# A fused attention and mixture-of-experts kernel: second products of three slots with w2 stationary, stored by output group

## The chip, the core and the metric

One core of one Trainium2 chip runs the whole program. The time is in device microseconds (us), and the number to beat is the median of three runs. Five engines work side by side, each through its own instructions in a fixed order: TensorE (PE), VectorE (DVE), ScalarE (ACT), GpSimd (POOL) and SyncE (SP), which here only issues DMAs. PEld is TensorE's weight load.

## The reference

The kernel computes attention with pooled queries and passes its result to a top-1 mixture of experts:

```
q_pool = q.reshape(B, H, S // 2, 2, D).mean(axis=3)      # B=8, H=8, S=1152, D=64
attn   = softmax(q_pool @ k^T / sqrt(D)) @ v
x      = attn as (4608 tokens, 512 features)
expert = argmax(x @ w_gate)                               # 8 experts
gate   = softmax(x @ w_gate)[expert]
out[token] = gate * (relu(x @ w1[expert]) @ w2[expert])   # w1: 512x1024, w2: 1024x512
```

## The kernel before, in words

**Stages.** The attention stage takes some 685 us: scores, exponentials, value products, and after each batch the routing, which writes every token into its expert's list in DRAM (a token number and its gate) and the token's 512 features into `x_runs`, cut into four runs of 128 features (each with 4 scale factors). Then come 16 expert slots, each one expert and up to 372 or 248 tokens: three early slots (31 places in each of 12 blocks), six wide slots with `PLACES` = 31, 29, 29, 27, 24, 24 places in each of 12 blocks of 32 (372, 348, 348, 324, 288 and 288 columns, in that order), and seven static slots with 31 places in 8 blocks (248 columns).

**A slot.** `tokens_of` loads the slot's piece of the list twice through GpSimd's queue (`re`, token and gate by output row, used by the store; `li`, from which `ix`, the indices of the runs, is made) and gathers the rows by indirect DMA, one GpSimd instruction per block, 12 in a wide slot and 8 in a static one (L1019). A gather waits for a mark, a group of matmuls of the slot two before, so that the gathers are spread over that slot. `turn_tokens` scales the rows on VectorE (`weigh`, L1198), turns them in 32 x 32 blocks (L1201), and splits the result into a high part (ScalarE, L1228) and a low part (VectorE, L1162), `xh` and `xl`. `split_weights` does the same for `w1` and `w2`, in four pieces of 1024 elements a partition each (L1245 and L1162). Every product is then three: high by high, high by low, low by high.

**First products** (L1288): a 128 x 128 block of `w1` is stationary, the slot's tokens move; 96 matmuls write the hidden values into `ph`, from where ScalarE makes `hh` (relu, L1296) and VectorE the low part `hl` (L1298). **Second products** (`second_products`, L1304 to L1337): for each group of 128 tokens a block of `hh` or `hl` is stationary and 512 columns of `w2` move; 24 matmuls for a group, 72 for a wide slot, 48 for a static one. ScalarE multiplies `py` by the gate into `y` (L1335), and GpSimd stores the 128 rows of 2 KB by one indirect DMA (L1327). There are two `ph` and two `py` banks, three `y` buffers, one `xh`/`xl`, and one buffer for each piece of the split weights.

**Order.** The program adds steps with a key, a duration and the buffers that they hold. `Flow.emit` plays them through a model (engines, two DMA queues, waits, buffers) and writes each engine's instructions in the order in which the model started them. `carry` adds an issuing step and a DMA step with a time of its own; in the model, DMA steps of GpSimd's queue (`DMA2`) pass one after the other, and a gather there takes 400 ns. On the chip each engine then keeps that order and waits at any instruction whose data is not there.

Of the kernel before, what the change touches and what calls it, by code (L numbers as in the profile page):

```python
# [9 lines left out]
F32 = mybir.dt.float32  # L10
# [9 lines left out]
EARLY = 3  # L20
PLACES = (31, 29, 29, 27, 24, 24)
WIDE = len(PLACES)
STATIC_SLOTS = 7
S_BUFS = 3
# [32 lines left out]
XR = 6  # L57
Y_BUFS = 3
DMA = 2000
# [203 lines left out]
def kernel(  # L263
# [173 lines left out]
    def act(n):  # L437
        return 110 + 0.833 * n

    def dve(n):  # L440
        return 67 + 1.042 * n
# [28 lines left out]
    def done(*steps):  # L470
        return [s for s in steps if s is not None]
# [483 lines left out]

    def tokens_of(o, f, key, tab, s, n, known, stored, early=False, m=None, steps=(), used=BU):

# [3 lines left out]
        x.n = x.nb * used  # L961
        x.whole = early
        x.re = tile_of(o, "rec2", [P, TW // P, 2], bufs=RE_BUFS)
# [10 lines left out]
        def load():  # L974


            src = lists[bass.ds(entry(tab, s, NE * LIST, ET_), n), :].rearrange("(i b) c -> i (b c)", b=x.nb)
            ins = [eng.dma_start(out=x.re.t[:x.rt, :x.nr].rearrange("p r c -> p (r c)"),
                                     in_=src[:x.u].rearrange("i (g r) -> g i r", g=NQD)),
# [47 lines left out]
        def mark(i):  # L1027
            return steps[i * len(steps) // x.nb] if steps else None

        p = f.carry(at, 2600, load, key - LEAD, [*known, *stored], [x.re, x.li], 120)  # L1030
        p = f.add("POOL", 250, index, key - LEAD, done(p), [x.li, x.ix])
        x.rows = done(*(f.carry("POOL", 1310, lambda i=i: gather(i), key + i * 3 / x.nb, done(p, mark(i) and mark(i).step, *stored), [x.ix, x.xr[i // NQD]], 400)
                        for i in range(x.nb)))
# [152 lines left out]
    def turn_tokens(o, m, f, x, key):  # L1186
# [4 lines left out]
        for r in range(x.nr):  # L1191
# [31 lines left out]

            p = f.add("DVE", dve(DM), weigh, key + r, x.rows[r * NQD:(r + 1) * NQD], [x.xr[r]])
            p = f.add("DVE", dve(DM), turn, key + r, done(p), [xt, x.xr[r]])
# [8 lines left out]
    def split_weights(m, f, x, kind, key, step, pool_bits):  # L1234
# [7 lines left out]
        for j in range(4):  # L1242
            src = lambda j=j: raw[j].t.rearrange("p (c f) -> p c f", c=NDC if one else 2)
            e = "POOL" if pool_bits >> j & 1 else "DVE"
            a = f.add("ACT", act(1024), lambda j=j, src=src: nc.scalar.copy(w[j].t[0], src()),  # L1245
                      key + step * j, done(got[j]), [raw[j], w[j]])
# [16 lines left out]
    def first_products(o, m, f, x, key):  # L1263
# [7 lines left out]
        for f0 in range(0, NFC, nb):  # L1271
            ph = hold_of("ph", lambda h: m.ps.tile([P, 512], F32, **h.own("ph")))
            view = lambda ph=ph: ph.t[:, :nb * n].rearrange("p (b t) -> p b t", b=nb)
            apart = lambda ph=ph: ph.t[:, :nb * n].rearrange("p (b t) -> p b t", t=x.rt)
            home = lambda i, f0=f0: blocks(hidden(m)[i])[:, f0 * x.nr:(f0 + nb) * x.nr, :x.rt]
            fs = slice(f0, f0 + nb)
# [27 lines left out]
    def second_products(o, m, f, x, key):  # L1304

        for r in range(x.nr):
# [30 lines left out]
            f.carry("POOL", 1300, scatter, at, done(a), [y, x.re], 1200)  # L1337


    with ExitStack() as cm, ExitStack() as units, ExitStack() as pairs:  # L1340
# [3 lines left out]
        def swap_units():  # L1344
# [4 lines left out]
                      fold=FOLD_BUFS, pa=1, sm=2, xT=2, rec=2, row=ROW_BUFS, lw=1, ex=1, de=1,  # L1349
                      ohb=1, di=2, re=2, rec2=RE_BUFS, li=LI_BUFS, ix=LI_BUFS, xr=XR, xq=XR2, xt=XT, raw=RAW, x=1, **{f"{w}{j}": 1 for w in ("w1", "w2") for j in range(4)}, **{f"h{c}": 1 for c in range(NFC)}, ph=2, py=2, px=2, y=Y_BUFS),  # L1350
                 ("kT", "qT", "vn", "fold", "s", "st"), ("x", "xt", "xq", *(f"{w}{j}" for w in ("w1", "w2") for j in range(4)), *(f"h{c}" for c in range(NFC)), "ph", "py", "px", "y"), swap_units)
        hold = []
# [36 lines left out]
        flag(o, f, key + K_SLOT + 20, [*outs, *table])  # L1389
        order = [(early, i, TW) for i in range(EARLY)] + [(wide, i, TW) for i in range(WIDE)]  # L1390
        order += [((etab, rtab), i, T) for i in range(STATIC_SLOTS)]
        base, marks = key + K_SLOT, []
        for i, (tab, s, n) in enumerate(order):
            at = base + SLOT * i
            experts, places_ = tab if isinstance(tab, tuple) else (tab[:, 0], tab[:, 1])
            if tab is early:
                x = first[s]
                known = done(x.found)
            else:
                x = tokens_of(o, f, at - AHEAD, places_, s, n, table, outs, m=m, steps=marks[i - 2],  # L1400
                              used=PLACES[s] if tab is wide else BU)
                known = table
# [81 lines left out]
```

## Time and profile before

| | us |
|---|---|
| median of 3 runs (lowest, highest) | 1145.75 (1144.46, 1146.11) |
| the profiled execution, its own time | 1139.45 |
| its span, first to last instruction | 1137.7 |
| mean granted TensorE clock in it | 0.995 |

The page of the profile gives each engine's busy share; windows and the chain of waits tell the stages apart. A busy TensorE is a matter of a model (matmuls overlap, and each one's end is modelled), so the pace of the matmuls is read from how many of them the chain passes in how long. "Idle before" at an instruction is the time in which its engine had nothing to run, and the name behind the arrow is what it waited for.

### The profile page before, as it was taken

The page shows a single profiled execution, that of the slowest core. Times are in us where ns is not written, and L with a number is a line of the kernel's source. Part 1 is how long each engine was busy: PE and PEld are TensorE (multiplying, and loading weights), DVE is VectorE, ACT ScalarE, POOL GpSimd, SP SyncE. Part 2 cuts the span into 40 slices and gives each one's busy share as a digit, 9 for nine tenths or more (in the row PEclk, how much of TensorE's full clock was granted, in tenths as well). Part 3 has the DMA queues.
Part 4 walks back from the last instruction along what each step waited for, and adds up shares of the span by engine and source line. Part 5 has one row for each costly group of instructions (what it writes and reads, how often), then busy time and mean ns, then how long its engine had stood idle before and what let it go on. Part 6 is the DMA issues. An engine that isn't in the chain of part 4 may idle for free.

```text
span 1137.7 us, 32922 instructions
## 1 busy us (share of the span) xinstructions
PE 1112.6 (98%) x13233; PEld 788.5 (69%) x13233; DVE 882.2 (78%) x2250; ACT 616.6 (54%) x831; POOL 849.5 (75%) x488
## 2 busy tenths in 40 slices
PE   7999999999999999999999999999999999999997
PEld 3555555565555565565665558988899989899986
DVE  6988998998989989989989839856555655667761
ACT  1656565565656656557556446444444444465551
POOL 1999899999999999999999852576576745445411
PEclk9999999999999999999999998999999999999999
DMA  9966866637557466567463427965556656577740
GB/s 132 154 130 101 143 96 107 128 68 126 106 86 130 84 110 115 86 110 122 73 108 87 113 63 203 234 186 163 161 178 191 199 167 188 191 229 256 248 157 30
DMA packets 398111, 158.07 MB, mean 139 GB/s; under 512 B 314454, under 2 KB 368626, under 8 KB 397950
## 3 DMA queue, kind: packets, MB, share of 16 engines
q1 hardware_dynamic: 378014, 133.93, 53.7%
q0 software_dynamic: 10464, 20.78, 6.0%
q10 hardware_dynamic: 9472, 1.18, 0.9%
q8 instruction: 106, 1.74, 0.7%
q14 instruction: 55, 0.45, 0.2%
HBM read 135.02 MB, written 22.07 MB: 138 GB/s over the span
## 4 chain that ended last, share of the span: by engine, by line
PE 75%; DVE 11%; issue 6%; DMA 3%; POOL 2%; ACT 1%; SPq 1%; POOLq 0%; DVEq 0%; ACTq 0%
PE st L572 20%; PE pa L708 19%; PE ph L1288 16%; PE py L1318 15%; DVE s L576 6%; PE st L654 2%; DMA vn<-in_v_dram 2%; DVE kT L536 1%; PE st L647 1%; DVE row L875 1%; ACT s L604 1%; DMA x_runs<-row 1%; SPq L484 1%; DMA kp<-in_k_dram 1%; POOL out_dram L1327 1%
## 5 line engine op out<-in xcount | busy, mean ns | idle before, releaser
L604 ACT ACTIVATE s<-s,bias 128x1152 f32<-128x1152 f32 (+1 forms) x320 | 352.1, 1152 | 243.5 <-DVE bias L600 235.4
L576 DVE TENSOR_SCALAR_CACHE_REDUCE s<-st 128x576 f32<-128x576 f32 x576 | 417.2, 748 | 41.7 <-PE st L572 26.9
L572 PE MATMUL st<-qT,kT 64*64 64x288 f32 x4608 | 366.1, 412 | 11.0 <-DVE kT L536 3.3
L708 PE MATMUL pa<-s,vn 64*64 64x288 f32 x4608 | 347.7, 404 | 0.3 <-ACT s L604 0.3
L572 PEld LDWEIGHTS st<-qT,kT 64*64 64x64 f32 x4608 | 165.2, 134 | 137.4 <-DVE s L576 47.2
L708 PEld LDWEIGHTS pa<-s,vn 64*64 64x64 f32 x4608 | 172.4, 133 | 106.6 <-DVE xT L715 7.5
L664 POOL TENSOR_TENSOR fold<-s 128x1728 f32<-128x1728 f32 x55 | 212.9, 3872 | 14.3 <-ACT s L604 13.6
L664 POOL TENSOR_TENSOR fold<-fold,s 128x1728 f32<-128x1728 f32 x55 | 213.2, 3877 | 1.6
L1288 PE MATMUL ph<-xh,w1h 128*128 128x248 f32 (+4 forms) x512 | 155.7, 304 | 2.7 <-DVE hl L1298 2.0
L1288 PE MATMUL ph<-xl,w1h 128*128 128x248 f32 (+4 forms) x512 | 154.9, 302 | 0.0
L1288 PE MATMUL ph<-xh,w1l 128*128 128x248 f32 (+4 forms) x512 | 154.2, 301 | 0.0
L1162 DVE TENSOR_TENSOR w2l<-raw,w2h 128x1024 fp32r<-128x1024 f32 x64 | 78.3, 1223 | 78.5 <-ACT w2h L1245 74.5
L1019 POOL DMA_INDIRECT xr<-x_runs,ix x76 | 92.3, 1215 | 50.4 <-issue 22.8
L1318 PE MATMUL py<-w2h,hh 128*128 128x512 f32 x328 | 128.1, 391 | 0.0
L1318 PE MATMUL py<-w2l,hh 128*128 128x512 f32 x328 | 127.8, 390 | 0.0
L1318 PE MATMUL py<-w2h,hl 128*128 128x512 f32 x328 | 127.8, 390 | 0.0
L1327 POOL DMA_INDIRECT out_dram<-y,rec x41 | 44.5, 1086 | 87.0 <-ACT y L1335 69.2
L1296 ACT ACTIVATE hh<-ph 128x372 fp32r<-128x372 f32 (+4 forms) x100 | 49.3, 493 | 110.8 <-PE ph L1288 110.8
L1288 PEld LDWEIGHTS ph<-xh,w1h 128*128 128x128 f32 x512 | 97.4, 190 | 5.2 <-DVE hl L1298 2.7
L1019 POOL DMA_INDIRECT xq<-x_runs,ix x52 | 61.3, 1178 | 50.0 <-PE py L1318 26.0
L1288 PEld LDWEIGHTS ph<-xl,w1h 128*128 128x128 f32 x512 | 97.3, 190 | 1.2 <-DVE xl L1162 0.4
L1288 PEld LDWEIGHTS ph<-xh,w1l 128*128 128x128 f32 x512 | 97.4, 190 | 0.0
(219 smaller groups left out, 1322.8 us busy)
## 6 DMA issues: line engine op xcount, KB each, us to landing
raw<-in_moe_w_dram SPq DMA_DIRECT2D x128, 512.0 KB
kp<-in_k_dram SPq DMA_DIRECT2D x124, 144.0 KB
vn<-in_v_dram SPq DMA_DIRECT2D x124, 144.0 KB
qn<-in_q_dram SPq DMA_DIRECT2D x120, 144.0 KB
x_runs<-row SPq DMA_DIRECT2D x96, 99.0 KB
xr<-x_runs,ix POOLq DMA_INDIRECT x76, 4.4
x_runs<-empty SPq DMA_DIRECT2D x4, 297.0 KB
qn<-in_q_dram ACTq DMA_DIRECT2D x16, 72.0 KB
```

Source lines behind the costliest of these rows:

```text
L572: nc.tensor.matmul(pt.t[to, h, :HQ], x.kT.t[up, c * P + i * D:c * P + (i + 1) * D], x.qT.t[up, cols], start=True, stop=True, tile_position ...
L576: nc.vector.tensor_scalar(s.t[:, c], pt.t[:, :, :HQ], -SCALE, None, op0=ALU.mult, op1=ALU.min, accum_out=mx.t[:, c:c + 1],)
L604: nc.scalar.activation(s.t[:, c0:c0 + n], s.t[:, c0:c0 + n], AF.Exp, bias=bias.t, scale=-1.0)
L654: nc.tensor.matmul(ps.t[to, 0, :HQ], ones4[:, hp, half, :], u.t[:, i, h], start=begin, stop=half == 1, tile_position=(0, to.start))
L664: add = lambda to, a, b: nc.gpsimd.tensor_tensor(to, a, b, ALU.add)
L708: mark.made = nc.tensor.matmul(pa.t[cs, i, :HQ], x.vn.t[up, h, c, :], s.t[up, c, h], start=c == 0, stop=c == NC - 1, tile_position=(up.sta ...
L1019: ins = nc.gpsimd.indirect_dma_start(out=x.xr[i // NQD].t[:, i % NQD, :], out_offset=None, in_=xg, in_offset=bass.IndirectOffsetOnAxis(ap= ...
L1162: (nc.gpsimd if eng == "POOL" else nc.vector).tensor_tensor(lo, raw, hi.bitcast(F32), ALU.subtract)
L1288: mark.made = nc.tensor.matmul(view()[:, i, :], a[:, c, fp], b[:, c, :n], start=c == 0 and k == 0, stop=c == NDC - 1 and k == 2)
L1296: a = f.add("ACT", act(nb * n) - 44, lambda home=home, apart=apart: nc.scalar.activation(home(0), apart(), AF.Relu), at - 20, done(p), [ph ...
L1318: mark.made = nc.tensor.matmul(py.t, blocks(a)[:, c * x.nr + r], b[:, c % 2, :], start=c == 0 and k == 0, stop=c == NFC - 1 and k == 2)
L1327: ins = nc.gpsimd.indirect_dma_start(out=out, out_offset=bass.IndirectOffsetOnAxis(ap=x.re.t.bitcast(I32)[:, r, 0:1], axis=0), in_=y.t, in ...
```

## The change

For the three smallest wide slots (`ACROSS` = 27 places and less) the second products turn round. A block of 128 columns of `w2` is stationary and the slot's hidden values move, for four chunks of 128 output features. The columns of `w2` are permuted when they are split, so that VectorE's 32 x 32 transposes leave, for each token, a contiguous run of 128 features in a partition; each block of 32 tokens is then stored with one indirect DMA of 128 runs of 512 bytes, by the index `ix` that the gathers used. The gate goes into the scale factors of the gathered rows instead (it is positive, so it passes through the relu), and these slots load no `re`. The wide slots run in the order `TURNS`, places 31, 24, 29, 24, 29, 27. A gather's DMA time in the planner's model goes from 400 to 1900 ns, for all slots but the early ones. There are two `y` buffers instead of three, and two buffers `yt` for the new form.

```
+TURNS = (0, 4, 1, 5, 2, 3)
+ACROSS = 27
-Y_BUFS = 3
+Y_BUFS = 2
+YT_BUFS = 2
...
-            ins = [eng.dma_start(out=x.re.t[:x.rt, :x.nr] ...
+            ins = [] if across else [eng.dma_start(out=x.re.t[:x.rt, :x.nr] ...
...
-        x.rows = done(*(f.carry("POOL", 1310, lambda i=i: gather(i), ..., [x.ix, x.xr[i // NQD]], 400)
+        x.rows = done(*(f.carry("POOL", 1310, lambda i=i: gather(i), ..., [x.ix, x.xr[i // NQD]], 1900)
...
+            def gates(r=r):
+                each = x.li.t[:, :x.nb].rearrange("p (g r) c -> p g r c", r=x.nr)[:, :, r, 1:2]
+                nc.vector.tensor_tensor(x.xr[r].t[:, :, P:], x.xr[r].t[:, :, P:], each.broadcast_to([P, NQD, NHP]), ALU.mult)
...
+            if x.across:
+                rows = done(f.add("DVE", 100, gates, key + r, rows, [x.xr[r], x.li]))
...
+            if not one and x.across:                       # split_weights, w2
+                groups = lambda t: t.rearrange("p (g c i) -> p c g i", g=NQD, c=NDC)
+                inner = lambda t: t.rearrange("p (c g i) -> p c g i", g=NQD, c=NDC)
+                steps = []
+                for i in range(2):
+                    a = f.add("ACT", act(512), lambda j=j, i=i, src=src: nc.scalar.copy(inner(w[j].t[0][:, i]), groups(src()[:, i])),
+                              key + step * j, done(got[j]), [raw[j], w[j]])
+                    d = f.add("DVE", dve(512), lambda j=j, i=i, src=src: low(
+                        "DVE", inner(w[j].t[1][:, i]), groups(src()[:, i]), inner(w[j].t[0][:, i])),
+                              key + step * j, done(a), [raw[j], w[j]])
...
+            home = lambda i, f0=f0: hidden(m)[i][:, f0:f0 + nb, :n] if x.across else \
+                blocks(hidden(m)[i])[:, f0 * x.nr:(f0 + nb) * x.nr, :x.rt]
...
+    def across_products(o, m, f, x, key):
+        y = hold_of("yt", lambda h: m.w.tile([P, TW // BL, NDC, BL], F32, **h.own("yt", YT_BUFS)))
+        runs = out.rearrange("t (g x) -> (t g) x", g=NQD)
+        n = x.n - x.u + BL
+        n += n % 2
+        turned = []
+        for d in range(NDC):
+            py = hold_of("py", lambda h: m.ps.tile([P, DM], F32, **h.own("py")))
+            at = key + 40.0 * d / NDC
+            p = None
+            for c0 in range(0, NFC, 2):
+                mark = Pools()
+                def product(d=d, c0=c0, py=py, mark=mark):
+                    (wh, wl), (hh, hl) = x.w2[c0 // 2].t, hidden(m)
+                    for c in (c0, c0 + 1):
+                        for k, (a, b) in enumerate(((wh, hh), (wl, hh), (wh, hl))):
+                            part = a[:, c % 2, d * P:(d + 1) * P]
+                            mark.made = nc.tensor.matmul(py.t[:, :n], part, b[:, c, :n],
+                                                         start=c == 0 and k == 0, stop=c == NFC - 1 and k == 2)
+                p = f.add("PE", 6 * n / 2.4 + 13, product, at + c0, ..., [py, x.w2[c0 // 2], *x.h[c0:c0 + 2]])
...
+            def turn(d=d, py=py):
+                t = py.t
+                each = bass.AP(tensor=t.tensor, offset=t.offset, ap=[list(t.ap[0]), [x.u, x.nb], [1, BL]])
+                nc.vector.transpose(y.t[:, :x.nb, d], each)
+            turned.append(f.add("DVE", dve(TW), turn, at, done(p), [py, y]))
+        def scatter(i):
+            place = i % NQD * x.nr + i // NQD
+            ins = nc.gpsimd.indirect_dma_start(
+                out=runs, out_offset=bass.IndirectOffsetOnAxis(ap=x.ix.t[:, place:place + 1], axis=0),
+                in_=y.t[:, i].rearrange("p c i -> p (c i)"), in_offset=None, bounds_check=NT * NQD - 1, oob_is_err=False,
+            )
...
+        for i in range(x.nb):
+            f.carry("POOL", 1300, lambda i=i: scatter(i), at + 40.0 * (i + 1) / x.nb, done(*turned), [y, x.ix], 1200)
...
-        order = [(early, i, TW) for i in range(EARLY)] + [(wide, i, TW) for i in range(WIDE)]
+        order = [(early, i, TW) for i in range(EARLY)] + [(wide, i, TW) for i in TURNS]
...
+                              used=..., across=tab is wide and PLACES[s] <= ACROSS)
-            second_products(o, m, f, x, at + 50)
+            (across_products if x.across else second_products)(o, m, f, x, at + 50)
```

## Rows read from the trace of the kernel before

**Rows 1.** The page's busy times: busy us, share of the span, instructions of each engine.

```profile
PE 1112.6 (98%) x13233; PEld 788.5 (69%) x13233; DVE 882.2 (78%) x2250; ACT 616.6 (54%) x831; POOL 849.5 (75%) x488
```

**Rows 2.** Windows cut at slot boundaries: stretch, length, busy times, clock, DMA share, GB/s.

```profile
790.12:822.50 32.38, 32.38 (x170) 29.52 (x170) 19.16 (x26) 15.34 (x22) 19.28 (x18) 1.00 0.56 179
...
917.20:949.75 32.55, 30.53 (x166) 27.20 (x165) 16.48 (x24) 14.09 (x22) 13.85 (x15) 0.95 0.56 171
949.75:978.81 29.06, 29.06 (x171) 26.20 (x170) 16.73 (x23) 14.20 (x21) 15.71 (x14) 1.00 0.61 185
...
1000.60:1131.00 130.40, 130.40 (x865) 119.03 (x863) 83.29 (x94) 67.56 (x87) 48.00 (x44) 1.00 0.59 192
```

**Rows 3.** The chain of waits in the expert stage: start, length, what, count.

```profile
790.12 16.01 PE ph L1288 x96
806.13 16.37 PE py L1318 x72
822.50 15.36 PE ph L1288 x96
...
885.91 10.89 PE ph L1288 x72
...
916.20 3.82 DMA xr<-x_runs,ix
...
923.72 6.55 PE ph L1288 x36
...
949.80 6.32 PE ph L1288 x48
...
978.81 10.89 PE ph L1288 x96
```

**Rows 4.** Timeline of TensorE around 920 us: start, length, instruction, idle before.

```profile
920.08 0.40 PE L1288 MATMUL ph<-xh,w1h 128*128 128x288 f32 x1 [0.23 <-DVE hl L1298]
...
923.72 0.40 PE L1288 MATMUL ph<-xh,w1h 128*128 128x288 f32 x1 [1.79 <-DVE hl L1298]
```

**Rows 5.** Timeline of VectorE in the same stretch.

```profile
922.61 0.69 DVE L1198 TENSOR_TENSOR xr<-xr 128x512 f32<-128x512 f32 x1 [2.58 <-issue]
```

**Rows 6.** Groups by line and shape, 650 to 1138 us: count | busy, mean ns | idle.

```profile
L1019 POOL DMA_INDIRECT xr<-x_runs,ix x76 | 92.3, 1215 | 50.4 <-issue 22.8 <-PE py L1318 19.2 <-PE ph L1288 5.6
L1162 DVE TENSOR_TENSOR w2l<-raw,w2h 128x1024 fp32r<-128x1024 f32 x64 | 78.3, 1223 | 78.5 <-ACT w2h L1245 74.5
...
L1245 ACT CAST w2h<-raw 128x1024 fp32r<-128x1024 f32 x64 | 67.1, 1051 | 19.4 <-PE py L1318 19.4
...
L1327 POOL DMA_INDIRECT out_dram<-y,rec x41 | 44.5, 1086 | 87.0 <-ACT y L1335 69.2 <-DVE w2l L1162 9.1 <-issue 3.6
...
L1335 ACT ACTIVATE y<-py,rec 128x512 f32<-128x512 f32 x41 | 28.3, 690 | 90.8 <-PE py L1318 81.3 <-issue 9.5
...
L1201 DVE STREAM_TRANSPOSE xt<-xr 128x512 f32<-128x512 f32 x19 | 13.4, 706 | 0.1
...
L1162 DVE TENSOR_TENSOR xl<-xt,xh 128x496 fp32r<-128x496 f32 x17 | 10.7, 669 | 0.0
...
L1228 ACT CAST xh<-xt 128x496 fp32r<-128x496 f32 x17 | 9.4, 603 | 0.5 <-DVE xt L1201 0.5
...
L798 DVE TENSOR_TENSOR lw<-pa,rec 96x64 f32<-96x64 f32 x6 | 0.9, 210 | 0.0
```

**Rows 7.** Timeline of GpSimd, from 817 us: start, length, instruction, idle before.

```profile
817.33 1.00 POOL L1019 DMA_INDIRECT xr<-x_runs,ix  x1 [1.68 <-PE py L1318]
818.63 1.03 POOL L1327 DMA_INDIRECT out_dram<-y,rec  x1 [0.30 <-issue]
820.05 1.66 POOL L1019 DMA_INDIRECT xr<-x_runs,ix  x1 [0.38 <-PE py L1318]
```

**Rows 8.** Line 1288's weight loads: duration in ns, min/median/max, first and last start.

```profile
L1288 PEld LDWEIGHTS ph<-xh,w1h x512: 186/188/334, 685.2 to 1119.8; 128*128 128x128 f32 x171
```

**Rows 9.** Line 1327's stores, 757 to 1131 us: from issue to landing.

```profile
DMA to landing us min/median/max: 2.7/4.3/6.5
```

More of the change, by code (lines that the diff above doesn't have):

```diff
@@ L961, in tokens_of @@
         x.n = x.nb * used
-        x.whole = early
+        x.whole, x.across = early, across
         x.re = tile_of(o, "rec2", [P, TW // P, 2], bufs=RE_BUFS)
@@ L977, in load @@
             src = lists[bass.ds(entry(tab, s, NE * LIST, ET_), n), :].rearrange("(i b) c -> i (b c)", b=x.nb)
-            ins = [eng.dma_start(out=x.re.t[:x.rt, :x.nr].rearrange("p r c -> p (r c)"),
+            ins = [] if across else [eng.dma_start(out=x.re.t[:x.rt, :x.nr].rearrange("p r c -> p (r c)"),
                                      in_=src[:x.u].rearrange("i (g r) -> g i r", g=NQD)),
@@ L1028, in mark @@
             return steps[i * len(steps) // x.nb] if steps else None
-        p = f.carry(at, 2600, load, key - LEAD, [*known, *stored], [x.re, x.li], 120)
+        p = f.carry(at, 2600, load, key - LEAD, [*known, *stored], [x.li] if across else [x.re, x.li], 120)
         p = f.add("POOL", 250, index, key - LEAD, done(p), [x.li, x.ix])
-        x.rows = done(*(f.carry("POOL", 1310, lambda i=i: gather(i), key + i * 3 / x.nb, done(p, mark(i) and mark(i).step, *stored), [x.ix, x.xr[i // NQD]], 400)
+        x.rows = done(*(f.carry("POOL", 1310, lambda i=i: gather(i), key + i * 3 / x.nb, done(p, mark(i) and mark(i).step, *stored), [x.ix, x.xr[i // NQD]], 1900)
                         for i in range(x.nb)))
@@ L1222, in turn_tokens @@
                 continue
-            p = f.add("DVE", dve(DM), weigh, key + r, x.rows[r * NQD:(r + 1) * NQD], [x.xr[r]])
+            rows = x.rows[r * NQD:(r + 1) * NQD]
+            if x.across:
+                rows = done(f.add("DVE", 100, gates, key + r, rows, [x.xr[r], x.li]))
+            p = f.add("DVE", dve(DM), weigh, key + r, rows, [x.xr[r]])
             p = f.add("DVE", dve(DM), turn, key + r, done(p), [xt, x.xr[r]])
@@ L1273, in first_products @@
             view = lambda ph=ph: ph.t[:, :nb * n].rearrange("p (b t) -> p b t", b=nb)
-            apart = lambda ph=ph: ph.t[:, :nb * n].rearrange("p (b t) -> p b t", t=x.rt)
-            home = lambda i, f0=f0: blocks(hidden(m)[i])[:, f0 * x.nr:(f0 + nb) * x.nr, :x.rt]
+            block = n if x.across else x.rt
+            apart = lambda ph=ph: ph.t[:, :nb * n].rearrange("p (b t) -> p b t", t=block)
+            home = lambda i, f0=f0: hidden(m)[i][:, f0:f0 + nb, :n] if x.across else \
+                blocks(hidden(m)[i])[:, f0 * x.nr:(f0 + nb) * x.nr, :x.rt]
             fs = slice(f0, f0 + nb)
@@ L1337, in second_products @@
             f.carry("POOL", 1300, scatter, at, done(a), [y, x.re], 1200)
+    def across_products(o, m, f, x, key):
[17 more added lines that the diff above has]
+                                                         start=c == 0 and k == 0, stop=c == NFC - 1 and k == 2)
+                p = f.add("PE", 6 * n / 2.4 + 13, product, at + c0, done(p, *x.w2_ready[c0 // 2], *x.made.get(c0, ()), *x.made.get(c0 + 1, ())),
+                          [py, x.w2[c0 // 2], *x.h[c0:c0 + 2]])
+                mark.step = p
+                x.marks.append(mark)
+            def turn(d=d, py=py):
[9 more added lines that the diff above has]
+            )
+            for other in m.stored:
+                tc.declare_no_dep(ins.ins, other.ins, reason="a token's row is stored once")
+            m.stored.append(ins)
+        for i in range(x.nb):
+            f.carry("POOL", 1300, lambda i=i: scatter(i), at + 40.0 * (i + 1) / x.nb, done(*turned), [y, x.ix], 1200)
@@ L1400 @@
                 x = tokens_of(o, f, at - AHEAD, places_, s, n, table, outs, m=m, steps=marks[i - 2],
-                              used=PLACES[s] if tab is wide else BU)
+                              used=PLACES[s] if tab is wide else BU, across=tab is wide and PLACES[s] <= ACROSS)
                 known = table
```

9 lines of the change are left out of this document (6 added, 3 removed).

## Prediction

> **What bounds the kernel now.** I read the page's busy times first. The reader should see that TensorE (PE) is busy 98% of the span, VectorE 78%, GpSimd 75% and ScalarE 54% [rows 1]. That average mixes the attention stage with the expert stage, and the change is in the expert stage only, so next come the windows, cut at the slot boundaries that the chain of waits shows. In the wide slot with 31 places PE is busy 32.38 of 32.38 us at a granted clock of 1.00, and over the last six static slots 130.40 of 130.40. One window differs: in the first 24-place slot PE is idle for 2.02 us and the granted clock's mean is 0.95 [rows 2]. The chain of waits agrees. From 779.9 to 978.8 us it runs nearly all on PE, piece after piece without a gap, and leaves PE once, over a gather and its landing at 916.20, to return at 923.72 [rows 3]. So in this stage PE's instruction stream is the time: what shortens the stream shortens the kernel, and other engines matter only where they make PE wait.
>
> The chain's pieces give the pace of one matmul, length divided by count [rows 3]. Moving 512 columns, the second products of today: 16.37 us for 72, 227 ns. The first products have the form that the change gives to the second ones (a weight block stationary, tokens moving): 372 columns 16.01/96 = 166.8 ns, 348 columns 15.36/96 = 160.0, 324 columns 10.89/72 = 151.3, 288 columns 6.32/48 = 131.7, 248 columns 10.89/96 = 113.4. Time goes down with columns right to the shortest row: 53.4 ns for 124 columns, 0.43 ns a column.
>
> **PE's own term.** In each slot of at most 27 places, 72 matmuls of 512 columns become 4 output chunks x 8 hidden chunks x 3 = 96. The columns moved are 12 x 27 - 27 + 32 = 329, made even, 330, and 12 x 24 - 24 + 32 = 296. For 296, from the nearest row (288): 131.7 + 8 x 0.43 = 135.1 ns, times 96 = 12.97 us in place of 16.37, so 3.4 saved. Ends: on the line from 248 to 372 it is 134.1 ns (3.5 saved), down from the 324 row 139.2 (3.0 saved). For 330, from the 324 row: 151.3 + 6 x 0.43 = 153.8 ns, 14.77 us, 1.6 saved; by the line 148.7 ns, 2.1 saved. Two slots of 24 and one of 27: 2 x 3.4 + 1.6 = **8.4 us saved**, ends 7.6 and 9.1. All of it is on the path, since PE has no idle time there to absorb it.
>
> These 96 matmuls bring 96 weight loads where there were 72, and a load's row reads 188 ns [rows 8], longer than the matmul it feeds. The first products of a static slot hold 96 such loads, 18.0 us of load time, in 10.89 us [rows 3, 8]; so loads overlap, and I add nothing for them. The Trainium skill speaks against that: "Perfetto Trace Analysis", Identifying the Most-Contended Engine, says that the share of time in weight loads, not in matmuls, tells how near TensorE is to its limit. Here that share is already 119.03 of 130.40 us, 91% [rows 2]. If loads set the pace, the new second products would take 96 x 0.188 = 18.0 us, 1.7 more than now; the static slots' row disagrees. This is a rival below.
>
> **The stall at 919 us.** The first products of the first 24-place slot should take 96 x 131.7 ns = 12.6 us. Before 920.08 and before 923.72 PE idled 0.23 and 1.79 us, both times for hl, the VectorE evacuation of ph [rows 4]. After the second wait 36 matmuls took 6.55 us, 182 ns each: 1.8 us lost [rows 3], at the lower of the two clock levels: a mean of 0.95 over 32.55 us is some 3.3 us at 1.2 instead of 2.4 GHz [rows 2]. With the waits that is 3.8 us; by the slot, 32.55 us against 29.06 for its twin, 3.5 [rows 2]. I use 3.6. The cause is order: on VectorE the weighing of the next slot's third row group stands between two evacuations and waited 2.58 us for its rows, whose last gather left GpSimd at 916.20 [rows 3, 5], though that slot needs them only 27 us later (it starts at 949.75). The change tells the planner that a gather takes 1.9 us to move instead of 0.4, so it will place weighings at least 1.5 us later, and it reorders the slots, so this meeting of instructions is not repeated as it stands. I take the 3.6 us as gone; the ends are 0 (the same blocking elsewhere) and 3.6.
>
> **VectorE and ScalarE, beside PE.** Per changed slot VectorE gains four transposes of 384 elements out of PSUM: a 512-element one from SBUF takes 706 ns, so 0.55 us by elements, at most 0.71 each, 2.2 us in all. Splitting w2 becomes 8 subtractions of 512 for 4 of 1024: 8 x 0.68 (the 496 row's 669 ns) against 4 x 1.223, 0.5 us more. Three tiny gate multiplications cost 0.15 each; the nearest small row is 210 ns, and the end below is zero; 0.5 us. Together 3.2 us [rows 6]. Today's 24-place windows hold 16.5 and 16.7 us of VectorE [rows 2], so about 20 in a slot of 12.6 + 13.0 = 25.6 us, 78%; the static slots run at 83.29 of 130.40, 64%, with no idle PE. ScalarE loses three y evacuations of 690 ns and gets 8 casts of about 0.61 for 4 of 1.051: 1.4 us less [rows 6]. The new wait is the transpose on PE's chunk. Behind it on VectorE stand the next slot's turning and splitting, and with two py banks PE needs a bank again one chunk after it finished it, 3.2 us later; today that is a row group, 5.4 us. That cover is thin, not gone. I charge each changed slot one wait like the smaller one of 920.08, 0.23 us idle and a slow restart, 0.4 us [rows 4]: **1.2 us**, ends 0 and 10.8 (a full stall of 3.6 us in each, rival 2's price).
>
> **GpSimd.** 3 scatters of a changed slot become 12: 9 x 1.086 us [rows 6] and the 0.30 us between neighbours [rows 7], 12.5 us more; one list load goes (also from SP's queue, which nothing waits for), taken as zero. Does it fit? A gather is 1.215 + 0.30 = 1.5, a scatter 1.39. The burst falls into the slot after a changed one. There: 12 gathers 18, 12 + 3 scatters 21, lists about 2, 41 us against 31.7 of PE: 9 us behind, regained in the next, shorter slot, which has 12 gathers and few scatters (20 + 9 = 29 against 25.6). After the 27-place slot a static slot has 8 gathers, 14 scatters and lists, 33.5 against 21.8: 12 us behind, regained at some 5 us a slot (10 x 1.5 + 2 = 17 against 21.8). Gathers are issued during the slot two before their own, and their rows are needed when their own begins, so rows 12 us late still arrive. Cost taken: nothing, covered by that lead; without it, the rival. The y buffers go from three to two. A y's store lands 4.3 us after its issue [rows 9], and the buffer is wanted again two row groups on, 10.9 us: covered, except while GpSimd is behind.
>
> Everything else is free: the order of the slots moves no PE work, and weights stream as before.
>
> **Sum.** Against the profiled execution (span 1137.7, its time 1139.45): - 8.4 - 3.6 + 1.2 = -10.8, 1128.65. The runs' median, 1145.75, lies 6.30 us above that execution; nothing in the trace says why, so I carry the difference over: **1134.95, say 1135**.
>
> **Rivals.**
> 1. The columns are saved but PE stalls of the old size (about 3.6 us) remain or move. For it: VectorE strictly in order, a weighing in front of evacuations, 78% load in the short slots. Against: the later placing. 1145.75 - 8.4 = 1137.4, with 1.2 at most 1138.6.
> 2. Stalls of several slots eat most of the saving: a full stall, 3.6 us, in two or three of them. 1137.4 + 3.6 to 7.2 = 1141 to 1144.6.
> 3. Slower: GpSimd's bursts reach PE. Place: the slots after the changed ones. The gathers and y scatters queued behind 12 scatters come 9 and 12 us late; a y without a free buffer stops ScalarE, and behind it the evacuations of ph. If both larger backlogs reach PE, +21 - 8.4 gives 1158; half of it, 1148. It decides once the delay passes the lead, about 15 us in the static slots (a slot's 21.8 less 3.8 of landing and some 3 of weighing, turning and splitting), that is once a GpSimd DMA costs 1.7 us with its gap, not 1.5. For it: some gathers take 1.66 [rows 7]. Against: the average already holds those.
> 4. Weight loads set the pace: 3 x 1.7 = 5 us instead of -8.4, 1147 with the old stall gone. The static row speaks clearly against it.
>
> **Chances.** Forecast, 1132 to 1136.5: 0.43. Rival 1: 0.29. Rival 2: 0.15. Rival 3: 0.11. Rival 4: 0.02. About 0.2% (2.3 us) is what a measurement of this kernel can tell from no change. Forecast, rival 1 and about half of rival 2 lie below 1143.46: faster 0.80; the rest of rival 2 and the milder part of rivals 3 and 4 give same 0.10; slower 0.10. The range 1130 to 1146 leaves out the bad half of rival 3 and the case in which the early slots' small stalls go too.
>
> **What would show it.** The py matmuls of the three slots as rows of 296 and 330 columns, 64 and 32 of each kind, at 135 and 154 ns from start to start, and a slot's second products of 13.0 and 14.8 us in the chain: near 227 x 72 again, or above, and the PE term is wrong. No half-clock stretch and no idle PE in the wide windows: the stall term right; PE waiting for hl behind a weighing: rival 1. PE waiting for py behind the transposes: my 1.2 us too small. GpSimd without idle time for a whole slot, and the chain leaving PE over gathers or scatters: rival 3. 68 scatters for 41. The forecast is wrong as a whole if PE's busy time falls by some 8 us and the time does not.

## The result, and the profile after

The changed kernel took 1154.86 us in the median of six runs (1150.79 to 1158.06), the kernel before beside it 1144.92 (1144.24 to 1146.11): a ratio of 1.0088, 95% interval [1.0071, 1.0104]. It is slower, where 1135 was forecast. That holds for the chip of these runs. On another chip, in the last experiments, the same two kernels took 1128.46 and 1137.79 us, a ratio of 0.991 [0.9885, 0.9934]: 9.3 us faster. Both results are the change's, and most of this section is what tells their profiles apart.

The page of the changed kernel on the first chip, its busy times, which answer to [rows 1]:

```profile
PE 1112.1 (97%) x13305; PEld 794.0 (69%) x13305; DVE 888.6 (77%) x2283; ACT 611.2 (53%) x834; POOL 876.1 (76%) x512
```

and on the chip of the last experiments (span 1126.5 us there, 1150.9 on the first):

```profile
PE 1102.4 (98%) x13305; PEld 785.8 (70%) x13305; DVE 888.2 (79%) x2283; ACT 610.8 (54%) x834; POOL 874.8 (78%) x512
```

Instructions are the same in number, and VectorE, ScalarE and GpSimd are as busy, within 1.3 us. PE's busy time is 9.7 us longer on the first chip, part of it matmuls at half the clock, as the windows show. The windows, cut at the slot boundaries of each trace's chain, say where the span grew. In order: the first 24-place slot, a 29, the second 24, the second 29, the 27, and the last six static slots (columns as in [rows 2]). The first chip:

```profile
831.09:856.97 25.88, 25.88 (x194) 25.77 (x194) 17.98 (x30) 12.57 (x21) 17.01 (x16) 1.00 0.62 196
856.97:889.90 32.93, 31.88 (x168) 28.39 (x168) 19.90 (x29) 14.46 (x24) 24.26 (x22) 1.00 0.56 169
889.90:923.51 33.61, 29.49 (x196) 28.62 (x195) 18.68 (x30) 13.15 (x23) 19.38 (x20) 0.90 0.58 173
923.51:962.28 38.77, 33.56 (x170) 30.40 (x170) 20.59 (x32) 15.22 (x25) 24.57 (x24) 0.91 0.48 149
962.28:991.08 28.80, 28.80 (x195) 28.80 (x194) 17.46 (x27) 12.78 (x20) 10.74 (x12) 1.00 0.55 178
1012.87:1143.50 130.63, 130.55 (x862) 118.94 (x862) 84.06 (x96) 67.52 (x87) 63.24 (x54) 1.00 0.61 197
```

The chip of the last experiments, the same kernel:

```profile
822.92:848.80 25.88, 25.88 (x194) 25.77 (x194) 17.94 (x30) 12.59 (x21) 17.01 (x16) 1.00 0.62 196
848.80:880.40 31.60, 31.60 (x170) 28.74 (x170) 20.51 (x31) 15.15 (x25) 23.97 (x22) 1.00 0.57 175
880.40:907.14 26.74, 26.12 (x195) 25.76 (x194) 17.90 (x30) 12.58 (x21) 21.40 (x20) 1.00 0.69 219
907.14:938.74 31.60, 31.60 (x170) 28.74 (x170) 20.51 (x32) 15.23 (x25) 24.78 (x23) 1.00 0.57 183
938.74:967.55 28.81, 28.81 (x195) 28.81 (x194) 17.46 (x27) 12.79 (x20) 12.11 (x14) 1.00 0.56 178
989.33:1119.72 130.39, 130.39 (x864) 119.03 (x863) 84.38 (x96) 67.60 (x87) 60.58 (x54) 1.00 0.61 197
```

The first, the fifth and the sixth rows agree to 0.3 us. The second, third and fourth are 1.3, 6.9 and 7.2 us longer on the first chip, 15.4 together. Two of them show a granted clock of 0.90 and 0.91: PE was idle, and behind that ran at 1.2 GHz for a stretch before it was back at 2.4. The first chip's chain of waits has the idle time itself, around 940 us:

```profile
844.73 12.24 PE py L1383 x90
...
932.57 3.83 PE ph L1313 x24
936.41 5.21 issue
941.61 5.67 PE ph L1313 x24
947.28 15.00 PE py L1343 x66
...
977.29 13.80 PE py L1383 x90
```

"Issue" names no releaser. But PE resumed 0.05 us after VectorE's `hl` had ended:

```profile
941.04 0.52 DVE L1323 SCALAR_TENSOR_TENSOR hl<-ph,hh 128x348 fp32r<-128x348 f32 x1 [6.98 <-issue]
```

`hl` needs `hh`, ScalarE's step on a finished first product, and PE can't reuse the bank `ph` before both. ScalarE, first chip:

```profile
931.28 0.46 ACT L1321 ACTIVATE hh<-ph 128x348 fp32r<-128x348 f32 x1 [1.46 <-PE ph L1313]
931.64 1.04 ACT L1268 CAST w1h<-raw 128x1024 fp32r<-128x1024 f32 x1
940.54 0.46 ACT L1321 ACTIVATE hh<-ph 128x348 fp32r<-128x348 f32 x1 [7.87 <-remote]
942.09 0.46 ACT L1321 ACTIVATE hh<-ph 128x348 fp32r<-128x348 f32 x1 [1.09 <-remote]
```

The same two `hh` on the chip of the last experiments:

```profile
918.14 0.46 ACT L1321 ACTIVATE hh<-ph 128x348 fp32r<-128x348 f32 x1 [1.90 <-PE ph L1313]
920.05 0.46 ACT L1321 ACTIVATE hh<-ph 128x348 fp32r<-128x348 f32 x1 [1.45 <-PE ph L1313]
```

On the first chip ScalarE was free at 932.7 and the product that it waited for ended by 934.5, yet it started at 940.54, 6.1 us later. I call a hand-off late when `hh` starts more than 0.8 us after both its product was finished and ScalarE was free. The first chip's trace has nine late ones, the other chip's trace of this kernel none, and the trace of before none.

An engine's signal, a semaphore update, tells the others that an instruction is done. "Remote" means that a signal was recorded just then and no instruction ended beside it that could have given it. The signal here is PE's own. Three first products ended at 934.49, 935.45 and 936.41; the trace records PE's signals for them at 940.46, 941.94 and 942.01. On the other chip the records of the same signals stand some 0.02 us behind the matmuls. So it was not ScalarE that was slow: PE's signal came late. In the traces of chips like the first, ScalarE's and VectorE's own signals stand within 0.15 us of their instructions, but for one or two at the program's end; only PE's are late. These traces also lack 149 to 232 of some 3,300 signal records of the three engines, the others at most 6, and the trace of before is one of the others by that.

GpSimd in the same places, first chip, a run of indirect DMAs without a pause (0.30 us is the usual gap):

```profile
934.10 0.98 POOL L1400 DMA_INDIRECT out_dram<-yt,ix  x1 [0.30 <-issue]
935.38 0.98 POOL L1400 DMA_INDIRECT out_dram<-yt,ix  x1 [0.30 <-issue]
936.67 0.98 POOL L1400 DMA_INDIRECT out_dram<-yt,ix  x1 [0.30 <-issue]
937.96 1.05 POOL L1022 DMA_INDIRECT xr<-x_runs,ix  x1 [0.30 <-issue]
939.32 1.01 POOL L1022 DMA_INDIRECT xr<-x_runs,ix  x1 [0.31 <-issue]
942.19 1.00 POOL L1022 DMA_INDIRECT xr<-x_runs,ix  x1 [1.87 <-remote]
```

This run began at 924.74 and paused after twelve DMAs, just as the late `hh` started. After 780 us the trace of before has no run of six or more; the changed kernel has runs of 17, 10, 12, 31 and 10 on the first chip, and of 33, 28, 31 and 10 on the other, with no late hand-off in them there.

### The profile page after: what moved, and what is told of

Same layout as the page of the kernel before. It is cut to its first block, busy times and chain, and to the rows that moved or that the text cites. A ratio compares the mean times of both kernels' runs of the same rounds, so it can differ in the third digit from the quotient of the medians.

```text
span 1150.9 us, 33093 instructions
## 1 busy us (share of the span) xinstructions
PE 1112.1 (97%) x13305; PEld 794.0 (69%) x13305; DVE 888.6 (77%) x2283; ACT 611.2 (53%) x834; POOL 876.1 (76%) x512
## 4 chain that ended last, share of the span: by engine, by line
PE 72%; DVE 15%; issue 7%; DMA 3%; POOL 1%; ACT 1%; SPq 1%; POOLq 0%; ACTq 0%; DVEq 0%
PE pa L711 19%; PE st L575 19%; PE ph L1313 15%; PE py L1343 11%; DVE s L579 7%; PE py L1383 3%; PE st L657 2%; DVE kT L539 1%; PE st L650 1%; DVE row L878 1%; DMA vn<-in_v_dram 1%; PE st L597 1%; DMA kp<-in_k_dram 1%; SPq L487 1%; DVE qT L543 0%
## 5 line engine op out<-in xcount | busy, mean ns | idle before, releaser
L575 PE MATMUL st<-qT,kT 64*64 64x288 f32 x4608 | 371.0, 412 | 13.5 <-DVE s L579 4.7
L711 PEld LDWEIGHTS pa<-s,vn 64*64 64x64 f32 x4608 | 175.7, 133 | 106.0 <-issue 7.9
L1022 POOL DMA_INDIRECT xr<-x_runs,ix x76 | 84.4, 1111 | 57.3 <-issue 22.6
L1165 DVE TENSOR_TENSOR w2l<-raw,w2h 128x1024 fp32r<-128x1024 f32 (+1 forms) x76 | 78.3, 1049 | 56.1 <-ACT w2h L1268 28.2
L1323 DVE SCALAR_TENSOR_TENSOR hl<-ph,hh 128x372 fp32r<-128x372 f32 (+4 forms) x100 | 55.5, 556 | 66.8 <-ACT hh L1321 46.0
L1343 PE MATMUL py<-w2h,hh 128*128 128x512 f32 x256 | 100.3, 392 | 1.0 <-issue 1.0
L1343 PE MATMUL py<-w2h,hl 128*128 128x512 f32 x256 | 99.9, 390 | 0.0
L1343 PE MATMUL py<-w2l,hh 128*128 128x512 f32 x256 | 99.8, 390 | 0.0
L1022 POOL DMA_INDIRECT xq<-x_runs,ix x52 | 58.4, 1122 | 42.1 <-PE ph L1313 11.8
```

Source lines behind the costliest of these rows:

```text
L575: nc.tensor.matmul(pt.t[to, h, :HQ], x.kT.t[up, c * P + i * D:c * P + (i + 1) * D], x.qT.t[up, cols], start=True, stop=True, tile_position ...
L711: mark.made = nc.tensor.matmul(pa.t[cs, i, :HQ], x.vn.t[up, h, c, :], s.t[up, c, h], start=c == 0, stop=c == NC - 1, tile_position=(up.sta ...
L1022: ins = nc.gpsimd.indirect_dma_start(out=x.xr[i // NQD].t[:, i % NQD, :], out_offset=None, in_=xg, in_offset=bass.IndirectOffsetOnAxis(ap= ...
L1165: (nc.gpsimd if eng == "POOL" else nc.vector).tensor_tensor(lo, raw, hi.bitcast(F32), ALU.subtract)
L1323: d = f.add("DVE", dve(nb * n), lambda home=home, apart=apart: nc.vector.scalar_tensor_tensor(home(1), apart(), 0.0, home(0).bitcast(F32), ...
L1343: mark.made = nc.tensor.matmul(py.t, blocks(a)[:, c * x.nr + r], b[:, c % 2, :], start=c == 0 and k == 0, stop=c == NFC - 1 and k == 2)
```

## The experiments

Ratios are to the kernel before, run beside it on the same chip. "The run" of an instruction is how many indirect DMAs GpSimd had issued without a longer pause when it was due. The chips come in two kinds by what the kernel before took on them: 1145 to 1147 us in the result above and in e1 to e12, 1138 in e13 to e18. The six chips of e1 to e18 were each used at one time only, so a "kind of chip" may also be a state that a chip was in.

**Which part of the change costs: e1, e2, e3, e4.**

```
e1: TURNS (0, 4, 1, 5, 2, 3) -> (0, 1, 2, 3, 4, 5); gather's move 1900 -> 400
e2: the kernel before with gather's move 400 -> 1900
e3: gather's move 1900 -> 400
e4: the changed kernel
```

> The new second products and stores alone: slots in the old order (31, 29, 29, 27, 24, 24 places), a gather at 400 ns in the planner. Theory S (the new form itself stalls the slots around it, with its 12 stores for 3): no gain, 1148 us or more, idle TensorE in the slots of 27, 24 and 24 places and in the one behind them. Theory O (the new order of the instructions, from the planner's 1900 ns and the alternation, does the harm): the columns are saved, about 1136 to 1138 us.

> The kernel before with nothing changed but the planner's time for a gather, 1900 ns instead of 400. Theory S: the stall of 3.6 us at 919 us goes or not, 1141 to 1145 us. Theory O: slower by 5 us or more, 1150 us, with stalls of TensorE in the wide slots.

> The changed kernel with the planner's gather time back at 400 ns (the new products, the alternation, two y buffers stay). Theory S: stalls stay, 1150 us or more. Theory O, by the gather time: 1137 us; theory O, by the alternation: 1150 us or more, as under S, and only the first experiment tells these two apart.

> The changed kernel once more, for a second trace of it. If its stalls are in the order of the instructions, TensorE is idle in the same places (before the first products of the second 24-place slot, and in the middle of those of the second 29-place slot), within 1 us, and the attention stage ends some 8 us later than in the kernel before. If they come from traffic that varies, the places and lengths differ: in all 1150 to 1158 us.

Measured: e1 1149.85 us, 1.0031 [1.001, 1.0053]; e2 1144.81, 0.9994 [0.9981, 1.0007]; e3 1152.48, 1.0053 [1.0029, 1.0076]; e4 1157.8, 1.0107 [1.0077, 1.0136]. The loss comes with the new second products, in each of these orders, but its size differs among them. The planner's 1900 ns alone costs nothing for the old products, and in e2's trace the stall of 3.6 us is gone from the wide slots:

```profile
PE ph L1288 <- DVE hl L1298: 0.5, 2, 0.2
```

Late hand-offs: e1 15, e2 none, e3 8, e4 11. e4's PE idles behind the matmuls that start at 876.5, 892.7, 896.1, 911.5, 934.9 and 939.7 us, the profile of the result behind 876.7, 893.0, 898.1, 912.5 and 936.1: much the same places, within 2 us, with other lengths; e4 has two more, at 939.7 and, 1.4 us long, at 1020.

**The products or the stores: e5, e6, e7.** e5 leaves nine of the twelve blocks of each changed slot unstored. e6 is the kernel before with nine gathers more in each of the three small slots, into a tile that nothing reads. e7 ties each slot's stores one by one to matmuls of the next slot.

```
e5: for i in range(x.nb): -> for i in range(3):          # the stores
e6: + for i in range(9 if extra else 0):
    +     f.carry("POOL", 1300, lambda i=i: first_again(i), at + 40.0 * (i + 1) / 12, done(p), [x.ix], 1200)
e7: + mark = marks[(2 * i + 1) * len(marks) // (2 * x.nb)] ...
    + behind(m.stored[-1], mark)
```

> The changed kernel with 3 of the 12 stores of each changed slot; the other nine blocks of these slots are left unstored. Theory B (GpSimd's unbroken runs of indirect DMAs make the hand-offs between engines late): with the count of before, the columns' saving shows whole, 1136 to 1139 us, and no evacuation of ph starts more than 0.8 us after TensorE has made it. Rival (the products, transposes or the order do it): 1150 us or more, as the changed kernel.

> The kernel before, its products and its order untouched, with nine more indirect DMAs on GpSimd after the second products of each of the three smallest wide slots: gathers of rows that are already there, into a tile that nobody reads. Theory B: slower by about what the changed kernel lost beside its saving, 1152 to 1160 us, with late evacuations in and after those slots. Rival (it is the writing of 512-byte runs, or the new products): 1143 to 1147 us, same as before.

> The changed kernel with each slot's 12 stores tied to groups of matmuls spread over the next slot, as the gathers are, so that GpSimd pauses between them. Theory B: shorter unbroken runs and fewer late hand-offs, 1137 to 1146 us. If GpSimd is simply too full in this stage (27 DMAs of some 1.3 us in 32 us), the runs stay as long and so does the time, 1150 us or more.

Measured: e5 1135.65 us, 0.992 [0.9899, 0.994]; e6 1156.8, 1.0108 [1.0089, 1.0127]; e7 1148.79, 1.003 [1.0016, 1.0043]. So the products, transposes, splits and order give the forecast's time to 0.7 us once three stores do the work of twelve, and nine indirect DMAs more in the three slots cost the old kernel 11.3 us, about the changed kernel's net loss (9.9 and 12.1). But e6's way is not the one that theory B expected: VectorE's waits name the weighing (line 1198), which then stands before evacuations.

```profile
DVE xr L1198 <- DMA xr<-x_runs,ix: 18.3, 6, 5.2
...
DVE xq L1198 <- DMA xq<-x_runs,ix: 7.9, 4, 2.9
```

In e2, the same products without the added gathers (and with the planner's 1900 ns), the first of these is:

```profile
DVE xr L1198 <- DMA xr<-x_runs,ix: 1.5, 1, 1.5
```

Late hand-offs: e5 two, by at most 1.1 us, e6 and e7 three each. So e6 shows a price of such DMAs by gathers that land late, which is rival 3's way, and not by late hand-offs. e7's time lies between its two forecasts: the marks did not break the runs. In it a hand-off 6.0 us late came at 893.1, 23 DMAs into a run.

**Stores moved to where GpSimd has room: e8, e9, e10.** e9's core, cut (e8 is its control, e10 has `ACROSS = 24`):

```
+        x.yx = tile_of(o, "yx", [P, TW // BL], I32, bufs=3) if across else None
...
+            if i < EARLY + WIDE - 2:
+                here = [a for a in spread if a[2] == i + 1] + [a for a in spread if a[2] == i + 2][:12]
+            else:
+                here = [a for a in spread if a[2] >= len(order) - 3][:-12]
```

> The changed kernel without the alternation (slots in the order 31, 29, 29, 27, 24, 24), all else as changed: 36 stores for 9, each slot's twelve behind its products. Control for the next two. Theory B (the number of indirect DMAs on GpSimd in the wide slots makes the loss): 1148 to 1153 us, since e1_across_only had the same order at 1149.85 and the planner's 1900 ns alone (e2_move_only) was worth nothing; late hand-offs (a first product's result taken up by ScalarE over 0.8 us after both were ready) several. Theory O (alternation with 1900 ns costs): 1140 or less.

> As e8, with the 36 stores moved in time and none left out: the 27-place slot's twelve are spread over the slot behind it and half of the next, the two 24-place slots' 24 over the last three static slots, where GpSimd was busy for 4.3 of 40 us in e1_across_only (its indices are kept in a tile of their own). Theory B: the column saving of 9.0 us comes through where GpSimd has room: 1135 to 1140 us, as e5_three_stores at 1135.65, with at most three late hand-offs. Theory S (twelve stores for three cost their time wherever they stand): 1148 to 1153, as e8.

> As e9 with only the two 24-place slots changed (the 27-place slot as before): 24 stores, all in the last three static slots. Saves 6.4 us of columns by the windows (2 x (29.06 - 25.88)). Theory B: 1137 to 1141 us. If the 27-place slot's stores still disturb in e9, this one is the faster of the two. Theory S: 1146 to 1150.

Measured: e8 1163.17 us, 1.0146 [1.0113, 1.0179], worse than any theory had it, with nine late hand-offs of up to 7.8 us; e9 1143.71, 0.998 [0.9964, 0.9997]; e10 1142.46, 0.9974 [0.9959, 0.9988]. e8 took 13.3 us more than e1, which differs only by the planner's 400 ns but ran on another chip: with the new stores the planner's order matters, and why is not shown. Moving the stores took back 20 us, but e9 and e10 missed their forecasts: five of e9's seven late hand-offs and all four of e10's lay with the moved stores, between 1065 and 1121 us, where none of the traces before had had one. That they follow the stores into another stage speaks for theory B.

**Stores between first products: e11, e12.** The 24 stores go behind second products only, of the last four static slots (six a slot) or of all seven (three or four).

```
e11: here = [a for a in spread if a[2] >= len(order) - 4][:-4]
e12: here = [a for a in spread if a[2] >= len(order) - 7][:-4]
```

> The two 24-place slots alone changed, as e10, with their 24 stores tied to second products only, those of the last four static slots, six to a slot, so that GpSimd's unbroken runs fall where TensorE hands nothing over to ScalarE but at the end of a block. So far the share of late hand-offs went by how many indirect DMAs GpSimd had issued without a pause: 4 of 670 up to the 4th, 25 of 104 from the 5th to the 8th, 41 of 73 behind that. Theory B: fewer late hand-offs than e10's four, and 1138 to 1141 us (6.4 us of columns off 1145.5). Theory S (the stores cost their time wherever they are): 1142 to 1146, as e10.

> As e11, the 24 stores spread over the second products of all seven static slots, three or four to a slot, where eight gathers a slot are still running in the first of them. Theory B: shorter runs, 1138 to 1141 us; if the gathers are pushed back by the stores instead, VectorE waits for them as in e6_nine_gathers, and the time is 1143 or more. Theory S: 1142 to 1146.

Measured: e11 1145.94 us, 0.9996 [0.9983, 1.0008], a miss for theory B and within theory S's range; e12 1137.18, 0.9917 [0.99, 0.9935], runs within 1136.21 to 1138.74, 0.8 us below theory B's range and against theory S. They differ only in the slots that the stores are spread over. In e11 stores and gathers joined to a run of 29, and 26 DMAs into it a hand-off was 4.2 us late; PE idled there for 2.9 us in four pieces. In e12 no hand-off was over 1.8 us late, and PE waited nowhere behind the first slot. Its runs were not short, as theory B had it: 22, 20 and 10 DMAs, gathers among the stores. So the length of a run alone does not say how late a hand-off is, and why e12's stay small is not shown. The chain of e12 over the two changed slots is nothing but PE:

```profile
930.99 6.35 PE ph L1315 x48
937.34 12.24 PE py L1385 x90
949.58 6.34 PE ph L1315 x48
955.92 0.82 PE py L1385 x6
956.74 6.35 PE ph L1315 x48
963.09 12.23 PE py L1385 x90
```

e12 beats the kernel before by 9.4 us on that chip, of which the columns explain 6.4 (the rest is not accounted for), and the changed one, which took 1.0088 and 1.0107 times the time of before on such chips, by some 20.

**What the run does, over all traces.** Each trace has 100 of these hand-offs. Counted by the run at the moment each was due, late ones of all:

| run | 1145 chips: the result's trace, e1 to e12 | 1138 chips: e13 to e18, and the trace of before |
|---|---|---|
| none | 1 of 377 | 0 of 217 |
| 1 to 4 | 6 of 730 | 1 of 389 |
| 5 to 8 | 25 of 107 | 0 of 60 |
| 9 to 12 | 24 of 45 | 0 of 11 |
| 13 and more | 22 of 41 | 0 of 23 |

On a 1145 chip a hand-off due five or more DMAs into a run is late in 71 of 193 cases, by up to 7.8 us; before the fifth in 7 of 1107, by at most 1.8. The list does not say whether the run makes the delay or both come of something third; that moving and leaving out stores moves and removes it (e5, e9, e10) speaks for the run. On the 1138 chips not one of 94 that deep in a run is late. The one late hand-off there, e15's, is of another sort: its `hh` waited for the slot before, whose second products still read the buffer, and PE idled for 0.2 us.

```profile
969.75 0.58 ACT L1323 ACTIVATE hh<-ph 128x496 fp32r<-128x496 f32 x1 [3.44 <-PE py L1385]
```

**The same sign in the attention stage.** The experiments change only the expert stage, but the traces kept show late signals before it too. From 20 to 660 us GpSimd issues 42 indirect DMAs, most of them 5 us or more apart, which move 0.03 of the stage's 69 MB (packets and MB in the first row; the first chip's trace):

```profile
q0 software_dynamic: 1344, 0.03, 0.2%
...
lists<-re,di POOLq DMA_INDIRECT x42
```

In the 13 traces of 1145 chips, 1953 of PE's recorded signals before 660 us fall within 3 us behind the start of one of these; 297 of them are more than 0.4 us late, by up to 1.2. Of the 7953 others none is, though SyncE's plain loads run through the whole stage. On the 1138 chips none of 5429 is late, near an indirect DMA or not. So a single small indirect DMA is enough on a 1145 chip, and there it is not the amount of traffic that does it.

**Traffic, GpSimd or the chip: e13, e14, e15, and e16, e17, e18.** In e13 and e14 nine of the twelve stores are plain DMAs to a scratch tensor; e15 is e12 with the 27-place slot changed too.

```
e13: + nc.sync.dma_start(out=there[i], in_=y.t[:, i].rearrange("p c i -> p (c i)"))
e14: + nc.gpsimd.dma_start(out=there[i], in_=y.t[:, i].rearrange("p c i -> p (c i)"))
```

> The changed kernel with nine of each changed slot's twelve stores made as plain DMAs of the same 128 x 512-byte blocks, issued by SyncE into a scratch tensor in DRAM (those nine blocks of the output are left unwritten, as in e5_three_stores); three stay indirect on GpSimd. Theory G (what makes the hand-offs late is GpSimd issuing many DMAs without a pause): 1135 to 1139 us, as e5 at 1135.65, few late hand-offs. Theory D (it is the stores' traffic to DRAM, whoever issues it): late hand-offs as after, 1150 to 1158 us.

> As e13, the nine plain DMAs issued by GpSimd. If it is the indirect form on GpSimd alone (theory I): 1135 to 1140 us, few late hand-offs, and shorter GpSimd runs if a plain issue is shorter than the 1.0 us of an indirect one. If any DMA from GpSimd does it (G): late hand-offs as after, 1146 to 1158. Theory D: 1150 to 1158, as e13.

> As e12_between_all (1137.18), with the 27-place slot changed too: its twelve stores spread over the slot behind it and the first products of the next, the 24-place slots' over the seven static slots' second products. Theory B: the 2.65 us of columns come off while the wide slots' GpSimd has room: 1134 to 1136 us; if its stores push the gathers or make hand-offs late there: 1138 or more.

> The changed kernel again, as control for the next two on one chip. The chip of e13 to e15 took 1137.86 us for the kernel before, where the others took 1145 to 1147, and no first product was late there in e13 and e14, so these two alone prove nothing on the cause. On a chip that takes 1145 for before: 1150 to 1158 us, late hand-offs as in after. On one that takes 1138 for before, either the same loss in proportion (ratio 1.005 to 1.013), or, if the late hand-offs are a matter of the chip, a gain (ratio about 0.99, 9 us).

> As e13_plain_sync (nine of each changed slot's twelve stores plain, by SyncE into a scratch tensor, those blocks of the output left unwritten), beside the changed kernel on one chip. Theory G (GpSimd issuing many DMAs without a pause makes hand-offs late): ratio 0.99 to 0.995 to before, hardly a late hand-off. Theory D (the stores' traffic does it): as e16.

> As e14_plain_gpsimd (the nine plain ones issued by GpSimd, 0.57 us each there against 1.0 to 1.2 for an indirect one), beside the changed kernel on one chip. Theory I (the indirect form alone): ratio 0.99 to 0.995, hardly a late hand-off, as e17. Theory G (any DMA from GpSimd): late hand-offs and a ratio over 1.0, between e17 and e16.

Measured, before at 1137.86: e13 1126.6 us, 0.9898 [0.9881, 0.9914]; e14 1128.26, 0.9913 [0.9897, 0.993]; e15 1127.61, 0.9911 [0.9895, 0.9928]. Before at 1137.79: e16, the changed kernel, 1128.46, 0.991 [0.9885, 0.9934]; e17 1126.86, 0.99 [0.9878, 0.9922]; e18 1128.48, 0.9916 [0.9893, 0.9939]. The ranges in us of e13 and e14 were meant for a 1145 chip. With e16 the case of a gain came: where no hand-off is late, nine indirect stores a slot cost 1.6 us more by the medians than plain ones by SyncE (e17), which the spread of the runs does not clear, and no more. These six therefore don't tell the stores' traffic from GpSimd's issuing on a 1145 chip. The attention stage above speaks for the issuing of indirect DMAs; for the stores themselves it stays open. e12 was not run on a 1138 chip, nor e15 on a 1145 chip.

## Why the prediction was wrong

**The columns were right.** Predicted 12.97 us for a 24-place slot's 96 products and 153.8 ns a product for the 27; the chain has 12.24 us for 90 (136.0 ns) and 13.80 for 90 (153.3). By the windows a 24-place slot went from 29.06 [rows 2] to 25.88 on either chip. For the 27-place slot this is the window of before, to hold against 28.80:

```profile
885.86:917.20 31.34, 31.34 (x175) 28.33 (x174) 19.08 (x26) 15.22 (x23) 21.08 (x18) 1.00 0.58 180
```

2 x 3.18 + 2.54 = 8.9 us against 8.4. Rival 4 is out: 96 loads of 188 ns, 18.0 us, stood in 13 us of products. The Trainium skill ("Perfetto Trace Analysis", Identifying the Most-Contended Engine) judges TensorE's headroom by the weight loads' busy share, beside the share of peak arithmetic. That share is 25.77 of 25.88 us in these windows, where PE had no headroom indeed; but the loads overlap, and the products kept the pace of their columns.

**The stall went, as predicted.** On the 1138 chip no window of the wide slots shows a clock below 1.00, and e2's trace had lost the stall by the 1900 ns alone. What it is worth is another matter: in e2's runs, on a 1145 chip, 0.7 us by the ratio and at most 2.2, not 3.6; no trace shows whether the kernel before stalls there on such a chip. **The new waits** were 0.9 us, not 1.2 (26.74 against 25.88): PE paused once, at 896.5 us in e16, for a `y` behind casts on ScalarE.

```profile
897.08 0.41 PE L1383 MATMUL py<-hh,w2h 128*128 128x296 f32 x1 [0.62 <-ACT y L1360]
```

**The sum** was right for the chip of its profile: from the first first-product to the last matmul the trace of before has 445.8 us and e16 435.3, 10.5 less against the 10.8 predicted; the profiled execution was put at 1128.65 and e16's took 1128.07. That these lie so close is in part luck: by the medians of that chip the change gained 9.3 us. The terms as measured, -8.9 - 3.5 + 0.9, give -11.5 where the stage lost 10.5; 1.0 us is not accounted for.

**The step that failed** is GpSimd's: "Cost taken: nothing, covered by that lead". The lead did cover the gathers: PE never waited for a row group in the profile after. But the step priced a burst only by what is queued behind it on GpSimd. On the first chip, with the burst, PE's signals to ScalarE come late, which do not pass through GpSimd at all, and the stage took 451.4 us where e16 took 435.3: 16.1 us for what was costed at nothing. The step's own working has a slip besides: 20 + 9 = 29 against 25.6 leaves 3.4 us behind, not "regained", before the next burst. e16's GpSimd did issue 33 indirect DMAs without a pause from 850.0 to 897.2 us, and on that chip nothing was late behind them. Rival 3 had the sign, the place and, with 1148 to 1158, the size, but another mechanism: gathers and `y` late by more than 15 us. Its waits appeared in e6, not here. It had a chance of 0.11.

**The sign that was there** is in the Sum: "nothing in the trace says why, so I carry the difference over". The 6.30 us between the profiled execution and the runs were no constant. The profile of before is one of a 1138 chip by its time (1139.45) and by its first first-product, at 685.2 us [rows 8], with e13 to e18 at 684.0 to 685.2, while every trace of a 1145 chip has it at 691 to 695 us with ScalarE's and GpSimd's instructions in the same order. The runs were of a 1145 chip. So no row of that profile could show a late hand-off; the range should have held the case that whatever made the runs 6 us longer also acts on the change. The 7 us of the attention stage are of the same sort: between e16 and the profile after, ScalarE's same instructions drift apart in small steps, by 1.0 us at 171, 2.2 at 320, 4.3 at 392, 6.4 at 488 and 8.3 at 661, and of the 7.6 us gained from 60 to 662 us, 7.3 lie within 5 us behind the start of one of the 42 indirect DMAs, in a third of the time. So the difference that was carried over as a constant stands where indirect DMAs are issued, and the change issues 27 more of them.

## What to carry to other kernels

When the profiled execution and the timed runs differ by more than the runs do among themselves, treat them as two machines: find the stage where they part before the difference is carried over, and take a second profile. A burst on one queue is to be priced by all that is under way while it lasts, not only by what stands behind it; moved to where little waits, the same work can cost nothing (e12 keeps the columns of two slots and spreads their 24 stores).

## What was not expected of the hardware

On chips that take 1145 us for the kernel before, `hh` starts up to 7.8 us late when GpSimd has issued five or more indirect DMAs without a pause (71 of 193), because PE's signal comes late; in the attention stage single ones delay it by up to 1.2 us. On chips that take 1138 us the same kernel with such runs shows no such delay (0 of 94). In two windows PE paused for 2.9 and 5.2 us and ran at 1.2 GHz behind that, seen as a granted clock of 0.90 and 0.91. Why the two kinds of chip differ, and how an indirect DMA holds up PE's signal, no run here shows. One rival is untested: every timed run was a recorded one, with a span and a clock of its own, and where signals are late some of their records are missing, so the delay may come with the recording.
